# TensorE's instruction pieces in the hand-made schedule of a retention layer with an MLP: visits placed by piece, one group at a time

## The chip, the core and the metric

The kernel runs on one core of a Trainium2 chip. The metric is the device time of one execution in microseconds (us); the time of a kernel is the median of its runs. Five engines work side by side and meet at semaphores: TensorE (PE in the profile, with its weight loads as PEld), VectorE (DVE), ScalarE (ACT), GpSimd (POOL) and SyncE (SP). Each carries out its own instructions in the order in which the program has them.

## The reference

Retention over 8 batches x 8 heads x 576 positions x 64 dimensions, then an MLP with an exact GELU over all 4608 tokens (512 -> 2048 -> 512). Inputs and output are float32; the kernel computes in bfloat16 with float32 sums.

```python
scores = scale * np.matmul(q, k.transpose(0, 1, 3, 2))
gamma = 1.0 - 2.0 ** (-5.0 - np.arange(H, dtype=np.float32))
rel = pos[:, None] - pos[None, :]
Dmat = np.where(rel >= 0, gamma[:, None, None] ** rel[None, :, :], 0.0)
attn = np.matmul(scores * Dmat, v)
x = attn.transpose(0, 2, 1, 3).reshape(B * S, H * D)
h = x @ w_in
out = (0.5 * h * (1.0 + erf(h / sqrt(2)))) @ w_out
```

## The kernel before

**Attention.** The sequence is cut into four chunks of 128 positions and a tail of 64. A *unit* is one chunk of one batch with all eight heads (the tails of two batches share one). The first four units are groups of their own; after them a *group* is two units, the same chunk of two batches, and a tail is a group too: 22 groups, 0 to 21. A group passes through four matmul steps, each of many small matmuls that use a part of TensorE's rows or columns:

- scores (`scores`, L559): 32 matmuls for a group; VectorE then multiplies the mask on (`masked`, L592)
- inner (`inner`, L646, tails L631): masked scores times v, 32 matmuls for a group (16 for a tail)
- state (`state`, L661): the sum over keys and values that the next chunk needs, 32 matmuls; VectorE and ScalarE keep it (L666 to L689)
- cross (`cross`, L711): q times the state of the chunk before, 32 matmuls, left out in chunk 0; VectorE then scales the result into x (`evacuate`, L735)

Inner, state and cross of a group together are a *visit* (`attend`). A visit may hold two groups: then the inner steps of both come first, their states next, their cross steps last. The planner ties two groups into one visit when they have the same chunk, from group `VISIT` on, and when the attention leads the MLP by more than `LEAD` units.

q and k must be turned before the scores. The groups in `BY_PE` (4 and 5, since `NPE = 2`) are loaded with positions on partitions, in 128 KB loads, and turned by TensorE: `turn`, 8 transposes for each of q and k (L494), then a copy out of PSUM. They need no second load of k. The groups in `BY_DVE` are loaded in four smaller loads for each of q and k (L342), turned by VectorE (`turn_dve`, L514) and, for q, put in order by ScalarE (`apart`, L525); their state step needs k once more, untransposed (`kn_ld`, L348). ScalarE scales v for all groups from 4 on (`scaled_v`, L609).

**MLP.** Tokens stand in 9 blocks of 512 = 4 units. The first product is plain for blocks 0 to 5 (`mlp1`, L758: matmuls of 128, 256 or 512 tokens) and a form with 7 products in place of 8 for blocks 6 to 8 (`mlp1_fast`, L972). The second product is plain for a part of block 0 (`mlp2`, L791) and has 7 products after it (`mlp2_fast`, L862: 8 matmuls of 256 columns per product). ScalarE applies the GELU; VectorE makes the sums that the 7-product forms need.

**The order.** All is one program without a loop on the chip. While it is built, a planner (the `while True` loop at the end) keeps a clock for each engine in `T`, with an assumed duration for each step, and at each moment takes a step whose inputs are there by these clocks: attention steps that are due first, then MLP work, which fills what is left. Attention steps are `A` (a visit), `AA` (a double visit), `U` (a state step by itself), `S` (scores) and `T` (transposes by TensorE). `AHEAD` and `RATE` bound how far scores may run ahead of the MLP, `SB`, `PER_G` and `PER_B` order VectorE's side jobs. So each engine's order is fixed when the program is built; on the chip an engine only waits.

Loads are issued by GpSimd in the order of the list `ORDER` (L374), and group by group after it (`reload`); stores by SyncE.

Of the kernel before, what the change touches and what calls it, by code (L numbers as in the profile page):

```python
# [17 lines left out]
def kernel(  # L18
# [14 lines left out]
    nc = tc.nc  # L33
# [35 lines left out]
    PLAIN = 4  # L69
    NPE = 2  # L70
    FAST1 = (5, 6, 7, 8)[PLAIN // 4:]
# [366 lines left out]
    def release(b, when):  # L438
        held.remove(b)
        free_at[b] = when  # L440

    def pe(dur, to="full"):
# [38 lines left out]
    def turn(n, jj):  # L481

        qk = loaded[groups[n][0]][0][jj]
        if n < 4:
            b, t = bank([128, HP, 128], BF16, "qk_ps")
            dst, m = turned(n, jj), HP
            for x in range(HP):
                nc.tensor.transpose(t[:, x], qk[:, 2 * x:2 * x + 2, :], ident1)
        else:
            b, t = bank([128, H, 128], BF16, "qk_ps")  # L490
            dst, m = turned(n, 1) if jj else qk.rearrange("p (h s) -> p h s", h=H), H
            for y in range(2):
                for hp in range(HP):
                    nc.tensor.transpose(t[:, y * HP + hp], qk[:, 4 * D * hp + y:4 * D * hp + 4 * D:2], ident1)  # L494
# [44 lines left out]
    def scores(n):  # L539
        g = groups[n]  # L540
        if n < 4:
            qT, kT = turned(n, 0), turned(n, 1)
            got = bank_pair(128)
            for hp in range(HP):
                for e in range(2):
                    sl = slice(64 * e, 64 * e + 64)
                    nc.tensor.matmul(got[1][:, e, hp, :], lhsT=kT[sl, hp, :], rhs=qT[sl, hp, :],
                                     start=True, stop=True)
            st[g[0]]["sc"] = got, pe(0.23, "row")
        else:  # L550
            short = len(g) == 1
            got = [bank_pair(TAIL if short else C) for _ in g]
            for hp in range(HP):
                for y in range(2):
                    for e in range(2):
                        for j in range(2):
                            sl = slice(64 * e + 32 * j, 64 * e + 32 * j + 32)
                            dst = got[0][1][64 * j:64 * j + 64, e, hp, :] if short else got[j][1][:, e, hp, :]
                            nc.tensor.matmul(dst, lhsT=turned_k(n, sl, hp, y), rhs=turned_q(n, sl, hp, y),  # L559
                                             start=(y == 0), stop=(y == 1), skip_group_check=True)  # L560
# [61 lines left out]
    def inner(i):  # L622
        bp, ci, j = units[i]
        s = st[i]
        if j is None:
            s["o"] = o = bank_pair(TAIL)
            for h in range(H):
                for jj in range(2):
                    sl, e = slice(64 * jj, 64 * jj + 64), 64 * (h % 2)
                    y = h // 2 + HP * (h % 2)  # L630
                    nc.tensor.matmul(o[1][e:e + 64, jj, h // 2, :], lhsT=s["vh"][sl, h, :], rhs=s["ret"][y // HP][sl, y % HP, :],  # L631
                                     start=(h < 2), stop=False, skip_group_check=True)
            s["B"] = pe(0.25, "quad")
            s_done.add(i)
        else:
            if i in raw:
                s["o"] = bank([128, HP, 128], FP32, "o_ps")
                o = s["o"][1]
            else:
                s["o"] = bank_pair(C) if j == 0 else st[i - 1]["o"]  # L640
                o = s["o"][1][:, j]
            vals = values(i) if i in raw else s["vh"]
            for hp in range(HP):
                for z in range(4):
                    e, d0 = z // 2, z % 2 * 32
                    nc.tensor.matmul(o[32 * z:32 * z + 32, hp, :], lhsT=vals[:, 2 * hp + e, d0:d0 + 32], rhs=s["ret"][e][:, hp, :],  # L646
                                     start=(hp == 0), stop=(ci == 0 and hp == HP - 1), skip_group_check=True)
            s["B"] = pe(0.27, "col4")
            if j == 1 and ci < NCI - 1:
                u_due.append((bp, ci))  # L650

    def state(bp, ci):
        pair = pair_of[bp, ci]
        b, u_ps = bank([128, H, D], FP32, "u_ps")
        for hp in range(HP):
            for y in range(2):
                for e in range(2):
                    for j, i in enumerate(pair):
                        h, p0 = 2 * hp + e, 64 * e + 32 * j
                        keys = loaded[i][0][1][:, h, y::2] if i < 4 else loaded[i][2][:, j, h, y::2]  # L660
                        nc.tensor.matmul(u_ps[p0:p0 + 32, 2 * hp + y, :], lhsT=keys, rhs=st[i]["vh"][:, h, :],  # L661
                                         start=(hp == y == 0), stop=(hp == HP - 1 and y == 1), skip_group_check=True)
# [36 lines left out]
    def cross(n):  # L699
# [6 lines left out]
        for hp in range(HP):  # L706
            for y in range(2):
                for e in range(2):
                    for j in range(2):
                        sl = slice(64 * e + 32 * j, 64 * e + 32 * j + 32)  # L710
                        nc.tensor.matmul(o[64 * e:64 * e + 64, j, hp, :], lhsT=u[sl, 2 * hp + y, :], rhs=turned_q(n, sl, hp, y),  # L711
                                         start=False, stop=(hp == HP - 1 and y == 1), skip_group_check=True)
# [41 lines left out]
    def mlp1(t, m0, n, lo, hi):  # L754
        b, hT = bank([128, n, hi - lo], FP32, "hT")
        for m in range(m0, m0 + n):
            for cc in range(N_DM):
                nc.tensor.matmul(hT[:, m - m0, :], lhsT=w_in[:, cc, m * 128:m * 128 + 128], rhs=x_tiles[t][:, cc, lo:hi],  # L758
                                 start=(cc == 0), stop=(cc == N_DM - 1))
# [25 lines left out]
    def mlp2(t, ts, m0, m1):  # L785
# [4 lines left out]
        for m in range(m0, m1):  # L790
            nc.tensor.matmul(oT, lhsT=g_of(t, ts // 2)[:, m, cols], rhs=w_out[:, m, :], start=(m == 0), stop=(m == N_DF - 1))  # L791
        done = pe((m1 - m0) * 0.2158)
# [58 lines left out]
    def mlp2_fast(t, p, name):  # L851
# [9 lines left out]
        for kk in range(HK):  # L861
            nc.tensor.matmul(dst, lhsT=x[:, kk, :], rhs=y[:, kk, :], start=(name in "125" and kk == 0),  # L862
                             stop=(kk == HK - 1), skip_group_check=True)
# [91 lines left out]
    def mlp1_fast(t, i, name):  # L955
# [13 lines left out]
        for m in range(2):  # L969
            for cc in range(HC):  # L970
                c0 = (2 * i + m) * 128
                nc.tensor.matmul(dst[:, m, :], lhsT=a[cc][:, c0:c0 + 128], rhs=y[:, cc, :],  # L972
                                 start=(name in "125" and m == 0 and cc == 0), stop=(cc == HC - 1), skip_group_check=True)
# [218 lines left out]
    def warm(n):  # L1192
        b, t = bank([128, 512], FP32, "warm")
        for _ in range(n):
            nc.tensor.matmul(t, lhsT=zeros[:, :128], rhs=zeros, start=True, stop=True)
        pe((0.32 if T["pe"] < HOT else 0.2158) * n)
# [34 lines left out]
    for _ in range(N_WARM):  # L1231
        b, t = bank([128, 512], FP32, "warm")
        nc.tensor.matmul(t, lhsT=zeros[:, :128], rhs=zeros, start=True, stop=True)
        release(b, 0.0)
    T["pe"] = 1.3 + 0.62 * N_WARM
    while True:
# [18 lines left out]
        if nB < nA:  # L1255
# [5 lines left out]
            if tied:  # L1261
                both = 1e9
                if nA > groups[n + 1][-1]:
                    both = max(ready, ready_for(n + 1))
                    acts.append((max(both, free_time(len(g) > 1 and units[g[0]][1] < NCI - 1, out_pairs(n, n + 1))), "AA"))
# [12 lines left out]
        if nT < 4 + NPE and nT <= group_of[min(nA, N_U - 1)] + 3 and (nT < 4 or not half or ring_free("tk")):  # L1278
# [99 lines left out]
```

## Time and profile before

| | |
|---|---|
| time, median of 3 runs | 292.36 us (291.45 to 294.36) |
| the profiled execution: time, span | 293.79 us, 292.0 us |
| TensorE busy | 277.5 us (95%), 4155 recorded matmuls |
| VectorE / ScalarE / GpSimd busy | 230.4 / 180.2 / 136.0 us |
| granted TensorE clock | full in all slices |
| loads (queue q0) | 21.12 MB, landing until 170.7 us |

In the profile "span" is the time from the first to the last instruction. A timeline line gives start and length in us, engine, source line, operation, what is written <- what is read, the shape and the number of instructions merged into it, and in brackets the idle time before it with its releaser. "issue" as a releaser means that the profile knows of nothing that the engine waited for. Matmuls overlap, so that a step is best measured from its start to the start of the next.

### The profile page before, as it was taken

The page shows a single profiled execution, that of the slowest core. Times are in us where ns is not written, and L with a number is a line of the kernel's source. Part 1 is how long each engine was busy: PE and PEld are TensorE (multiplying, and loading weights), DVE is VectorE, ACT ScalarE, POOL GpSimd, SP SyncE. Part 2 cuts the span into 40 slices and gives each one's busy share as a digit, 9 for nine tenths or more (in the row PEclk, how much of TensorE's full clock was granted, in tenths as well). Part 3 has the DMA queues.
Part 4 walks back from the last instruction along what each step waited for, and adds up shares of the span by engine and source line. Part 5 has one row for each costly group of instructions (what it writes and reads, how often), then busy time and mean ns, then how long its engine had stood idle before and what let it go on. Part 6 is the DMA issues. An engine that isn't in the chain of part 4 may idle for free.

```text
span 292.0 us, 9753 instructions
## 1 busy us (share of the span) xinstructions
PE 277.5 (95%) x4155; PEld 212.3 (73%) x4179; DVE 230.4 (79%) x380; ACT 180.2 (62%) x407; POOL 136.0 (47%) x205
## 2 busy tenths in 40 slices
PE   6979998999899999999799999999999999999994
PEld 2468766888747666665666766767888888888883
DVE  5564387899959579877797898988996998899851
ACT  7456558579778687679477596744545455556421
POOL 8956867989899777787785900000000000000000
PEclk9999999999999999999999999999999999999999
DMA  9999999999999999999999750201010202101114
GB/s 154 170 188 191 195 154 211 185 151 127 144 108 120 126 191 148 164 131 186 131 129 175 61 93 3 57 21 72 2 74 0 75 0 75 72 2 72 38 54 127
DMA packets 109131, 31.96 MB, mean 109 GB/s; under 512 B 85792, under 2 KB 104736, under 8 KB 109088
## 3 DMA queue, kind: packets, MB, share of 16 engines
q0 software_dynamic: 100400, 21.12, 82.6%
q1 hardware_dynamic: 7184, 9.44, 9.8%
q10 hardware_dynamic: 1504, 0.79, 1.0%
q8 instruction: 32, 0.52, 0.7%
q14 instruction: 11, 0.09, 0.1%
HBM read 42.99 MB, written 9.44 MB: 180 GB/s over the span
## 4 chain that ended last, share of the span: by engine, by line
PE 89%; POOL 4%; DMA 3%; issue 2%; ACT 0%; DVE 0%; POOLq 0%
PE psum L862 36%; PE psum L758 27%; PE psum L972 13%; DMA early<-in_v_dram 3%; PE psum L559 3%; PE psum L646 3%; PE psum L711 3%; PE psum L791 2%; POOL early L364 2%; PE psum L661 1%; POOL w_in L307 1%; PE psum L494 1%; PE psum L631 0%; POOL w_out L322 0%; ACT x L453 0%
## 5 line engine op out<-in xcount | busy, mean ns | idle before, releaser
L758 PE MATMUL psum<-x,w_in 128*128 128x512 bf16 (+2 forms) x547 | 89.7, 307 | 2.8 <-issue 1.7
L758 PEld LDWEIGHTS <-w_in 128*128 128x128 bf16 x568 | 49.8, 98 | 24.1 <-issue 1.2
L862 PEld LDWEIGHTS <-g_all 128*128 128x128 bf16 x544 | 52.3, 98 | 12.8 <-issue 2.0
L763 ACT ACTIVATE g_all<-psum 128x512 bf16<-128x512 f32 x64 | 37.6, 594 | 28.2 <-PE psum L758 28.2
L862 PE MATMUL psum<-w_out,g_all 128*128 128x256 bf16 x408 | 52.0, 273 | 1.9 <-issue 1.8
L862 PEld LDWEIGHTS <-s 128*128 128x128 bf16 x408 | 39.5, 98 | 8.8
L342 POOL DMA_DIRECT2D k_ld<-in_k_dram x64 | 35.2, 567 | 18.4 <-DMA q_ld<-in_q_dram 7.8
L609 ACT ACTIVATE vh<-v_ld,dv 128x128 bf16<-128x128 bf16 (+1 forms) x144 | 42.2, 380 | 0.0
L977 ACT ACTIVATE g_all<-t 128x512 bf16<-128x512 f32 x36 | 22.6, 630 | 29.0 <-DVE t L985 28.9
L592 DVE TENSOR_TENSOR ret<-psum,msk 128x1024 bf16<-128x1024 f32 (+1 forms) x32 | 35.6, 1150 | 3.0 <-PE psum L559 2.5
L342 POOL DMA_DIRECT2D q_ld<-in_q_dram x64 | 35.1, 566 | 1.8 <-DMA q_ld<-in_q_dram 0.9
L862 PE MATMUL psum<-wt,s 128*128 128x256 bf16 x272 | 34.1, 273 | 0.0
L848 DVE TENSOR_TENSOR o_sb<-psum,t 128x256 f32<-128x256 f32 x51 | 21.5, 421 | 14.9 <-PE psum L862 6.0
L453 ACT COPY t<-psum 128x256 f32<-128x256 f32 (+1 forms) x46 | 20.0, 435 | 17.1 <-PE psum L862 13.4
L985 DVE TENSOR_TENSOR t<-psum,t 128x512 f32<-128x512 f32 x36 | 24.7, 689 | 6.0 <-ACT t L453 4.2
L972 PE MATMUL psum<-x,w_in 128*128 128x256 bf16 x192 | 25.9, 273 | 0.0
L451 DVE COPY t<-psum 128x512 f32<-128x512 f32 (+1 forms) x41 | 22.7, 559 | 3.7 <-PE psum L862 3.6
L766 ACT ACTIVATE g_all<-psum 128x512 bf16<-128x512 f32 (+1 forms) x39 | 19.1, 523 | 10.4 <-PE psum L758 9.8
L735 DVE TENSOR_TENSOR x<-psum,dqT 128x1024 bf16<-128x1024 f32 (+1 forms) x18 | 19.3, 1099 | 2.1 <-PE psum L711 2.1
L972 PEld LDWEIGHTS <-w_in 128*128 128x128 bf16 x192 | 18.8, 98 | 2.4
L972 PE MATMUL psum<-x,ws 128*128 128x256 bf16 x144 | 19.5, 273 | 0.0
L353 POOL DMA_DIRECT2D v_ld<-in_v_dram x14 | 16.3, 1164 | 3.5 <-DMA kn_ld<-in_k_dram 1.3
(107 smaller groups left out, 371.4 us busy)
## 6 DMA issues: line engine op xcount, KB each, us to landing
out_dram<-o_sb SPq DMA_DIRECT2D x31, 256.0 KB, 2.3
v_ld<-in_v_dram POOLq DMA_DIRECT2D x14, 256.0 KB, 5.6
q_ld<-in_q_dram POOLq DMA_DIRECT2D x48, 64.0 KB, 5.1
k_ld<-in_k_dram POOLq DMA_DIRECT2D x48, 64.0 KB, 4.2
kn_ld<-in_k_dram POOLq DMA_DIRECT2D x12, 256.0 KB, 6.4
w_in<-in_moe_w_in_dram POOLq DMA_DIRECT2D x8, 256.0 KB, 8.4
w_out<-in_moe_w_out_dram POOLq DMA_DIRECT2D x8, 256.0 KB, 9.2
q_ld<-in_q_dram POOLq DMA_DIRECT2D x4, 128.0 KB, 9.2
```

The costliest lines, as they stand in the source:

```text
L342: nc.gpsimd.dma_start(qk["qk".index(what)][p0:p0 + 32, 0:HP * per].rearrange("p (h x) -> p h x", h=HP), {"q": q, "k": k}[what][2 * bp + jj ...
L451: nc.vector.tensor_copy(dst, src)
L453: nc.scalar.copy(dst, src)
L592: nc.vector.tensor_tensor(both.rearrange("p (e h) s -> p e h s", e=2), t, by, op=ALU.mult)
L609: nc.scalar.activation(vh[:, 0:m, h], src[:, :, h], AF.Copy, scale=dv[:, h, ci:ci + 1])
L758: nc.tensor.matmul(hT[:, m - m0, :], lhsT=w_in[:, cc, m * 128:m * 128 + 128], rhs=x_tiles[t][:, cc, lo:hi], start=(cc == 0), stop=(cc == N ...
L763: nc.scalar.activation(g_all[:, t % 2, :, m0, :], hT.rearrange("p n (a c) -> p (n a) c", a=2), AF.Gelu)
L848: nc.vector.tensor_tensor(dst, src, f[key], op=ALU.add)
L862: nc.tensor.matmul(dst, lhsT=x[:, kk, :], rhs=y[:, kk, :], start=(name in "125" and kk == 0), stop=(kk == HK - 1), skip_group_check=True)
L972: nc.tensor.matmul(dst[:, m, :], lhsT=a[cc][:, c0:c0 + 128], rhs=y[:, cc, :], start=(name in "125" and m == 0 and cc == 0), stop=(cc == HC ...
L977: nc.scalar.activation(g_of(t, part)[:, m0:m0 + 2], src, AF.Gelu)
L985: nc.vector.tensor_tensor(f[key], f["b"][1], f[key], op=ALU.add)
```

## The change

The planner gets a model of how TensorE's instructions come. It counts the instructions (`mm` and `mm_turn` stand for the matmul and transpose calls, 2.004 instructions each), takes them to come in pieces of 256 whose edges lie at 194 plus a multiple of 256, and takes a piece to be there `FETCH` = 5.0 us after the piece before it was begun. From 20 us on, its TensorE clock `pe` stands still at an edge until then, and a visit or a score step that would cross an edge is not due before that time (`fetch_at`). These are waits in the planner's clock: no wait instruction is added to the program; another step takes the place.

With it come other constants: one more group is turned by TensorE (`NPE` 3), no visit holds two groups (`VISIT` 30 is past the last group), one more warm-up matmul in each early gap (`WPLUS`), other bounds for how far the attention runs ahead and for the side jobs, and a new `ORDER` of the loads. In the program that results TensorE has 4188 matmuls and transposes in place of 4179.

```diff
-    NPE = 2
+    NPE = 3
-    VH_POOL = 30
+    VH_POOL = 16
-    AHEAD = 14
-    RATE = 3.8
+    AHEAD = 13
+    RATE = 4.4
-    STATE10 = 20.0
+    STATE10 = 24.0
+    FETCH = 5.0
-    WPLUS = 0
-    VISIT = 8
-    LEAD = 2.0
+    WPLUS = 1
+    VISIT = 30
+    LEAD = 5.0
-    SLACK, SB, PER_G, PER_B, TURN0 = 1.2, 9.0, 6.0, 40.0, 0.0
+    SLACK, SB, PER_G, PER_B, TURN0 = 1.2, 5.0, 10.0, 30.0, 0.0
...
-    ORDER = ("wi0 io k2 q1 k1 wi7 q2 v1 k3 wi1 wo2 v0 wi6 q3 v2 wi5 wi3 wi2 v3 q4 wi4 wo1 wo0 wo4 wo7 wo6 wo3 wo5 "
-             "k4 q5 v4 k5 q6 dq2 k6 k7 q7 v6 q8 q9 k8 n4 n8 k9 q10 v8 q11 dq3 n6 k11 q12 k10 v10 n10 q13 k13 dq4 "
-             "n12 k12 v12 dq0").split()
+    ORDER = ("wi0 io k2 q1 k1 wi7 q2 v1 k3 wi1 wo2 v0 wi6 q3 v2 wi2 wi5 wi3 v3 wi4 q4 wo1 wo0 wo4 wo3 wo7 wo6 wo5 "
+             "k4 q5 n4 v4 k5 q6 dq2 k6 k7 q7 q8 q9 v6 k8 n8 k9 q10 v8 dq3 n6 k11 k10 q11 q12 n10 v10 q13 k13 dq4 "
+             "n12 v12 dq0 k12").split()
...
+    count = [3.0, 3.0]
+    piece = [0.0]
+
+    def mm(*a, **k):
+        count[0] += 2.004
+        nc.tensor.matmul(*a, **k)
...
+    def place(n):
+        return (n - 194.0) // 256, (n - 194.0) % 256
+
+    def fetch_at(n):
+
+        at = place(count[0])[1]
+        wait = piece[0] + FETCH - (256 - at) * 0.0075 if at + n >= 256 else 0.0
+        return 0.0 if T["pe"] < 20.0 else wait
+
+    def one_piece(n):
+        return place(count[0])[1] + n < 512
+
     def pe(dur, to="full"):
...
-        T["pe"] += dur * (2.0 if T["pe"] < HOT else 1.0)
+        dur *= 2.0 if T["pe"] < HOT else 1.0
+        new, old = place(count[0])[0], place(count[1])[0]
+        if new > old:
+            turn_at = T["pe"] + dur * (1 - place(count[0])[1] / max(1.0, count[0] - count[1]))
+            wait = max(0.0, piece[0] + FETCH - turn_at) if T["pe"] > 20.0 else 0.0
+            piece[0] = turn_at + wait
+            T["pe"] += wait
+        count[1] = count[0]
+        T["pe"] += dur
         return T["pe"] + DRAIN
...
-                if nA > groups[n + 1][-1]:
+                if nA > groups[n + 1][-1] and one_piece(384 if len(g) > 1 else 192):
...
-                acts.append((max(ready, free_time(n < 4, out_pairs(n))), "A"))
+                acts.append((max(ready, fetch_at(192 if n >= 4 else 0), free_time(n < 4, out_pairs(n))), "A"))
...
-                acts.append((max(s_ready(), free_time(0, len(g))), "S"))
+                acts.append((max(s_ready(), fetch_at(64 if n >= 4 else 0), free_time(0, len(g))), "S"))
```

More of the change, by code (lines that the diff above doesn't have):

```diff
@@ L440, in release, with mm_turn @@
         free_at[b] = when
+    count = [3.0, 3.0]
[3 more added lines that the diff above has]
+        nc.tensor.matmul(*a, **k)
+    def mm_turn(*a, **k):
+        count[0] += 2.004
+        nc.tensor.transpose(*a, **k)
+    def place(n):
[6 more added lines that the diff above has]
+        return place(count[0])[1] + n < 512
     def pe(dur, to="full"):
@@ L487, in turn @@
             for x in range(HP):
-                nc.tensor.transpose(t[:, x], qk[:, 2 * x:2 * x + 2, :], ident1)
+                mm_turn(t[:, x], qk[:, 2 * x:2 * x + 2, :], ident1)
         else:
@@ L493, in turn @@
                 for hp in range(HP):
-                    nc.tensor.transpose(t[:, y * HP + hp], qk[:, 4 * D * hp + y:4 * D * hp + 4 * D:2], ident1)
+                    mm_turn(t[:, y * HP + hp], qk[:, 4 * D * hp + y:4 * D * hp + 4 * D:2], ident1)
         done = pe(0.056 * m)
@@ L630, in inner @@
                     y = h // 2 + HP * (h % 2)
-                    nc.tensor.matmul(o[1][e:e + 64, jj, h // 2, :], lhsT=s["vh"][sl, h, :], rhs=s["ret"][y // HP][sl, y % HP, :],
+                    mm(o[1][e:e + 64, jj, h // 2, :], lhsT=s["vh"][sl, h, :], rhs=s["ret"][y // HP][sl, y % HP, :],
                                      start=(h < 2), stop=False, skip_group_check=True)
@@ L645, in inner @@
                     e, d0 = z // 2, z % 2 * 32
-                    nc.tensor.matmul(o[32 * z:32 * z + 32, hp, :], lhsT=vals[:, 2 * hp + e, d0:d0 + 32], rhs=s["ret"][e][:, hp, :],
+                    mm(o[32 * z:32 * z + 32, hp, :], lhsT=vals[:, 2 * hp + e, d0:d0 + 32], rhs=s["ret"][e][:, hp, :],
                                      start=(hp == 0), stop=(ci == 0 and hp == HP - 1), skip_group_check=True)
@@ L757, in mlp1 @@
             for cc in range(N_DM):
-                nc.tensor.matmul(hT[:, m - m0, :], lhsT=w_in[:, cc, m * 128:m * 128 + 128], rhs=x_tiles[t][:, cc, lo:hi],
+                mm(hT[:, m - m0, :], lhsT=w_in[:, cc, m * 128:m * 128 + 128], rhs=x_tiles[t][:, cc, lo:hi],
                                  start=(cc == 0), stop=(cc == N_DM - 1))
@@ L790, in mlp2 @@
         for m in range(m0, m1):
-            nc.tensor.matmul(oT, lhsT=g_of(t, ts // 2)[:, m, cols], rhs=w_out[:, m, :], start=(m == 0), stop=(m == N_DF - 1))
+            mm(oT, lhsT=g_of(t, ts // 2)[:, m, cols], rhs=w_out[:, m, :], start=(m == 0), stop=(m == N_DF - 1))
         done = pe((m1 - m0) * 0.2158)
@@ L861, in mlp2_fast @@
         for kk in range(HK):
-            nc.tensor.matmul(dst, lhsT=x[:, kk, :], rhs=y[:, kk, :], start=(name in "125" and kk == 0),
+            mm(dst, lhsT=x[:, kk, :], rhs=y[:, kk, :], start=(name in "125" and kk == 0),
                              stop=(kk == HK - 1), skip_group_check=True)
@@ L1194, in warm @@
         for _ in range(n):
-            nc.tensor.matmul(t, lhsT=zeros[:, :128], rhs=zeros, start=True, stop=True)
+            mm(t, lhsT=zeros[:, :128], rhs=zeros, start=True, stop=True)
         pe((0.32 if T["pe"] < HOT else 0.2158) * n)
@@ L1232 @@
         b, t = bank([128, 512], FP32, "warm")
-        nc.tensor.matmul(t, lhsT=zeros[:, :128], rhs=zeros, start=True, stop=True)
+        mm(t, lhsT=zeros[:, :128], rhs=zeros, start=True, stop=True)
         release(b, 0.0)
```

12 lines of the change are left out of this document (6 added, 6 removed).

## The prediction

> **What bounds the kernel now.** I read the page first (busy shares and the chain that ended last), then the waits of TensorE, then its timeline around each wait, then the DMA queues and the landings of the loads.
>
> ```profile
> span 292.0 us, 9753 instructions
> PE 277.5 (95%) x4155; PEld 212.3 (73%) x4179; DVE 230.4 (79%) x380; ACT 180.2 (62%) x407; POOL 136.0 (47%) x205
> ...
> q8 instruction: 32, 0.52, 0.7%
> ...
> PE 89%; POOL 4%; DMA 3%; issue 2%; ACT 0%; DVE 0%; POOLq 0%
> ```
>
> TensorE is the chain: 89% of the span, and busy for 277.5 of 292.0 us. The rest of the chain is the start: a load of v that lands at 20.97 us releases the chain, and from there TensorE alone sets the time. Nearly the only thing on the chain after that is "issue", a stop with no releaser that the profile knows. The timeline of TensorE shows three of them:
>
> ```profile
> 48.01 0.35 PE L711 MATMUL psum<-q_ld,u_sb 32*64 32x128 bf16 x10
> 49.64 0.52 PE L711 MATMUL psum<-q_ld,u_sb 32*64 32x128 bf16 x22 [1.27 <-issue]
> ...
> 80.11 1.24 PE L758 MATMUL psum<-x,w_in 128*128 128x512 bf16 x5 [0.76 <-issue]
> ...
> 137.99 1.08 PE L646 MATMUL psum<-ret,vh 128*32 128x128 bf16 x64
> 138.90 0.70 PE L661 MATMUL psum<-vh,kn_ld 128*32 128x64 bf16 x64
> 139.53 1.09 PE L711 MATMUL psum<-q_ld,u_sb 32*64 32x128 bf16 x64
> 140.54 1.37 PE L862 MATMUL psum<-w_out,g_all 128*128 128x256 bf16 x11
> 143.76 0.71 PE L862 MATMUL psum<-w_out,g_all 128*128 128x256 bf16 x5 [1.84 <-issue]
> ```
>
> Together 1.27 + 0.76 + 1.84 = 3.87 us. Each lies in the middle of a run of equal matmuls, so no operand can be late. The instruction queue q8 explains them: 32 packets, 0.52 MB, so 16 KB each, over 8,334 recorded loads and matmuls of TensorE, one packet per 256 or so. Counted through the program's order, the stops fall on multiples of 256 instructions (plus 194), and in each case a packet landed shortly before: at 48.12 (work resumes at 49.64), 78.44 (80.11) and 142.52 (143.76). So TensorE waits for its next piece, and resumes 1.2 to 1.7 us after its packet has landed. Since one packet starts per edge passed, a piece must last as long as the next one takes to come. From edge to resumption the three took 5.5 (44.13 to 49.64), 4.6 (75.47 to 80.11) and 4.7 us (139.06 to 143.76). The attention is what empties pieces fast: the visit at 137.99 runs 192 matmuls, one and a half pieces, in 2.55 us, where 128 matmuls of L862 take 14 us.
>
> The Trainium skill ("Runtime: NRT & Kernel Launch", section "Instruction fetch mechanics") says that instructions come in 16 KiB blocks of 256 by a DMA queue of the sequencer, and that crossing into the next is mostly hidden. The block size agrees with the 16 KB packets here; "hidden" does not: 3.87 us are not. By that rule the first term below would be nothing, and the sum 294.3 instead of 291.7; it is a rival below, worked out from rows.
>
> **The change, term by term.** The order of the instructions of the changed program tells what moved. From the step at 202.1 us (first L972) to the end TensorE's order is the same in both; up to the v load of 20.97 us the loads have the same order, so this landing still pins the start (one warm matmul more and a shifted one fall into the 1.07 us that TensorE idles there). What changes lies between 22.1 and 202.1 us. I price each run of matmuls by its start-to-start time in the timeline: 0.109 us for a 256-wide matmul, 0.216 for a 512-wide, 0.056 for a 128-wide or a transpose, 0.56 for the 32 matmuls of a score step (L559), and 0.10 for entering attention work from full-size matmuls (a run of 8 of L862 lasts 0.97 instead of 0.87 before it). Summed so, the order of before ends at 283.6 us, the record at 287.9: the difference, 4.3, is the 3.87 of stops and 0.4 of rounding, so the prices hold.
>
> *1. The stops of before go: -3.87.* Scores and visits are now put only where a piece has had 5 us by the planner's clock, and double visits are gone.
>
> *2. New stops: +1.35.* In the new order, summed with the same prices, no piece is shorter than 4.76 us; twelve lie between 4.76 and 5.9 while loads still run. What a piece needs I take from all 18 edges of before between 44 and 165 us, as packet's landing plus 1.5 us minus TensorE's passing of the edge: from 1.1 to 6.7 us, ten of them above 4.2, five above 5.1. Averaging the shortfall over these 18 for each of the twelve gives 0.23 us for the shortest, 0.13 for one of 5.1, 0.05 for one of 5.7; the sum is 1.35. Bounds: nothing, if the slow packets meet long pieces, and 3.9 if the packets come late as often as they hurt before. I take 1.35, since the readings are of this kernel under the same loads.
>
> *3. Two more transposes by TensorE (NPE 3): +0.90.* The third group now has q and k turned by TensorE, 2 x 8 matmuls. The row:
>
> ```profile
> 39.01 0.61 PE L494 MATMUL psum<-ident,q_ld 128*128 128x128 bf16 x8
> 39.45 1.46 PE L791 MATMUL psum<-w_out,g_all 128*128 128x512 bf16 x6
> ```
>
> 39.01 to 39.45 is 0.45 each. They are on the chain in full. What they save is not: two stream transposes of VectorE (0.94 us mean each) and a 1.04 us copy of ScalarE, against two copies from PSUM (0.7 to 1.0 us); nine DMA issues of GpSimd (8 x 0.57 + 1.17 = 5.7 us) become four (4 x 0.88 = 3.5). VectorE and ScalarE never wait for a load after 26 us, so TensorE's work hides all of it. The DMA engines gain little: 1024 packets of 512 bytes at 62 ns and 2048 of 128 bytes at 32 give 129 us over 16 engines, 4096 of 128 bytes 131. By landings the old form took 5.3 us (46.38 to 51.70), four loads of the new form 3.0 (at 0.75 each, 42.08 to 44.32). Later loads come 1 to 2 us earlier.
>
> *4. Single visits: +1.28.* A single visit against half a double one:
>
> ```profile
> 75.17 0.63 PE L646 MATMUL psum<-ret,vh 128*32 128x128 bf16 x32
> 75.63 0.42 PE L661 MATMUL psum<-vh,kn_ld 128*32 128x64 bf16 x32
> 75.97 0.64 PE L711 MATMUL psum<-q_ld,u_sb 32*64 32x128 bf16 x32
> 76.55 1.05 PE L862 MATMUL psum<-wt,g_all 128*128 128x256 bf16 x8
> ```
>
> Two singles: 2 x (76.55 - 75.17) + 2 x 0.10 = 2.95. One double: 140.54 - 137.99 + 0.10 = 2.65. So 0.30 each for the three doubles with L711, 0.18 for the one without (1.81 against 1.63), 0.10 for each of the two tail pairs: 0.90 + 0.18 + 0.20.
>
> *5. Places of scores, chunk sizes: +0.08.* Two entries more from full-size work, one fewer elsewhere (+0.10); eight 256-wide matmuls of the first block replace sixteen 128-wide (-0.02). VH_POOL has no effect, since ScalarE scales v for every later group.
>
> The other loads' new order costs nothing if the loads still come in time, so that is the cover to test. By the sum the attention now runs 2 to 12 us earlier: the scores of the first late group at 98.8 instead of 105.9, a later one at 117.6 instead of 126.3. Their loads landed in before at 93.1 and 111.1, so 5.7 and 6.5 us remain, plus the 1 to 2 us of term 3. Before itself ran a score step 5.8 us after its last load (51.70 to 57.48) without a wait. Two turns on VectorE (2 x 1.13) and ScalarE's copy (1.04) need 3.3 us. The tightest new place is the k transpose of the third group, 50.6 us by the sum: q of it should land at 45.8, v of the second at 47.9, its own k at 49.4 (0.75 a load, 2.06 for v). With 1.03 a load, the longest of that run, it is 50.5. No queue is moved past another: GpSimd issues all loads in both, SyncE's stores stay.
>
> Sum: -3.87 + 1.35 + 0.90 + 1.28 + 0.08 = -0.26, span 291.7. The profiled execution took 293.79, 1.79 around its span, 1.43 above the median of 292.36. Against the median: 292.1.
>
> **Rivals.**
> *A. The waits do not take the stops away.* Either the stops are no fetches, or packets come 1 us later than the plan thinks. For it: readings above 5 us are five of 18, and the 6.7 one stood right behind a visit. Against it: all three stops lie on piece edges. Then 3.9 us stay and 2.26 are added: 292.36 + 2.3 = 294.7.
> *B. Slower: a score step meets its loads.* The loads are paced by the DMA engines (digit 9 in the page's DMA row until 165 us), and by packet time the third group's cost them the same as before. If the landings do not move and the chain of VectorE and ScalarE takes 8 to 9 us as a rule (the other scores with VectorE's turns had 7.5 us and more in before), the score steps at 73 to 118 us, several of them with 5.7 to 6.5 us, wait 2 to 3 us, once, as all later work shifts with them. It decides from a lead under about 6 us; VectorE, standing in the same wait, holds up the sums queued behind. 292.1 + 3 = 295.1. Against: the lead of 5.8 that was enough.
> *C. Faster: no piece is late at all*, and TensorE's order ends as summed: 292.36 - 3.87 + 2.26 = 290.7; with the 0.4 of rounding also gained, 290.3. For it: most pieces have over 5.4 us, and late in the kernel the packets come within 3.6 us.
>
> **How the numbers follow.** Forecast 0.54, A 0.14, B 0.17, C 0.15. A measurement of this kernel can tell about 1%, 2.9 us. The forecast (290.8 to 293.7 by the bounds of terms 2 and 3) stays within it but for 0.03 on either side; A by 0.11 of its 0.14; B is beyond for 0.12; C for 0.09. So faster 0.12, same 0.70, slower 0.18. The range 289.6 to 295.0 leaves out the far ends of B and C.
>
> **What would show it.** Right: TensorE's busy time up by about 2 us, "issue" waits under 2 us in total, visits of 32 matmuls each in about 1.5 us with the entry, L494 with 48 matmuls, first L972 at about 202 us, q8 with 32 or 33 packets. Wrong: "issue" stops of 3 us or more (A), score steps or their turns waiting for DMA (B), a chain in which the first L972 comes before 199.5 us or after 205.

## The result: 294.85 us, slower by 0.6%, and the profile after

| | before | after |
|---|---|---|
| time, median of 10 runs each | 293.02 us (291.45 to 295.83) | 294.85 us (293.41 to 296.92) |
| ratio, 95% interval | | 1.006 [1.0034, 1.0087] |
| the profiled execution: time, span | 293.79, 292.0 us | 294.77, 293.0 us |
| TensorE busy | 277.5 us | 280.9 us |

The change is within the 1% that the prediction took as the least that a measurement can tell, but its interval lies clear of 1: the kernel became slower by about 1.8 us (1.0 to 2.5), where a gain of 0.3 us was forecast. (The median of before from ten runs is 0.66 us above the one from three that the prediction started from.) Ratios, and the counts of timed executions further down, leave out the few that took over 1.5% longer than the fastest of the same kernel.

The page of the changed kernel, the lines that answer to those of before:

```profile
span 293.0 us, 9764 instructions
...
PE 280.9 (96%) x4159; PEld 213.7 (73%) x4188; DVE 224.8 (77%) x375; ACT 182.5 (62%) x410; POOL 133.9 (46%) x200
...
PEclk9989999999999999999999999999999999999999
...
q8 instruction: 32, 0.52, 0.7%
...
PE 90%; DMA 3%; POOL 3%; issue 1%; DVE 1%; ACT 0%; POOLq 0%
```

TensorE is still the chain, and busy for 3.4 us more. "issue" went from 2% of the chain to 1%, but VectorE, which had 0%, has 1% now. The third digit of the clock row fell to 8; in before all were 9. The waits of TensorE (columns: engine, tile and line, releaser, then us in total, times, longest) say which waits these are. In the changed kernel every matmul carries L449 and every transpose L453, the lines of the two helpers, so one has to go by tiles and times:

```profile
PE psum L449 <- DMA w_in<-in_moe_w_in_dram: 2.2, 1, 2.2
...
PE psum L449 <- DVE ret L625: 1.1, 1, 1.1
PE psum L449 <- issue: 0.6, 4, 0.2
```

Of the stops without a releaser, 3.87 us in three places in before, none is left: the 0.6 us are four gaps of at most 0.2 us, and gaps of 0.16 us stand in before as well. So the change did what it says. But a wait of 1.1 us for VectorE's masked scores (`ret`) is new, and the longest wait is one of 2.2 us for a load of w_in in the first 20 us. The new wait in the timeline of TensorE, inside the visit of the second double-unit group:

```profile
48.66 0.62 PE L449 MATMUL psum<-q_ld,kT 32*128 32x128 bf16 x32
...
50.19 0.63 PE L449 MATMUL psum<-ret,vh 128*32 128x128 bf16 x32
51.94 0.42 PE L449 MATMUL psum<-vh,k_ld 128*32 128x64 bf16 x32 [1.11 <-DVE ret L625]
52.28 0.64 PE L449 MATMUL psum<-q_ld,u_sb 32*64 32x128 bf16 x32
```

50.19 to 51.94 is 1.75 us for an inner step that takes 0.46 elsewhere: 1.29 us lost, at nearly the place where before lost its 1.27 (the cross step at 49.64). The start of the kernel, as windows (us of the window, then busy time and number of instructions of PE, PEld, DVE, ACT, POOL, then granted clock, DMA share and GB/s):

```profile
16.40:19.80 3.40, 1.23 (x16) 0.99 (x15) 0.00 (x0) 1.74 (x4) 1.20 (x3) 1.00 1.95 177
19.80:23.20 3.40, 3.29 (x43) 2.49 (x41) 1.97 (x4) 1.18 (x2) 2.64 (x4) 0.50 1.51 193
```

In the first window TensorE does 1.23 us of work in 3.40, since it stands for the third chunk of w_in; in the second the granted clock is half.

**The sum from the trace.** I cut the span of TensorE in three: the *start*, up to the first plain matmul run after the fourth single-unit score (22.11 us in before); the *middle*, up to the first L972; and the rest. The middle is again priced by start-to-start rows, and what it lasted above its price is the *excess*, that is, stops and waits. From the first L972 to TensorE's last matmul both kernels take 85.75 us.

| us | before | after | difference | forecast |
|---|---|---|---|---|
| start | 22.11 | 22.69 | +0.58 | 0 |
| middle, priced work | 175.86 | 178.11 | +2.25 | +2.26 |
| middle, excess | 4.15 | 2.24 | -1.91 | -2.52 |
| the rest | 85.75 | 85.75 | 0 | 0 |
| sum | | | +0.93 | -0.26 |

The agreement of the priced work is no test of the prices: the same prices were put on the same order before and after the result. The excess takes up whatever they have wrong, in this table and in the experiments. A split that needs no prices, and by which the work did not come out, follows the experiments.

### The profile page after: what moved, and what is told of

Same layout as the page of the kernel before. It is cut to its first block, busy times and chain, and to the rows that moved or that the text cites. A ratio compares the mean times of both kernels' runs of the same rounds, so it can differ in the third digit from the quotient of the medians.

```text
span 293.0 us, 9764 instructions
## 1 busy us (share of the span) xinstructions
PE 280.9 (96%) x4159; PEld 213.7 (73%) x4188; DVE 224.8 (77%) x375; ACT 182.5 (62%) x410; POOL 133.9 (46%) x200
## 4 chain that ended last, share of the span: by engine, by line
PE 90%; DMA 3%; POOL 3%; issue 1%; DVE 1%; ACT 0%; POOLq 0%
PE psum L449 89%; DMA w_in<-in_moe_w_in_dram 3%; POOL early L365 2%; PE psum L453 1%; POOL w_in L308 1%; DVE ret L625 1%; POOL w_out L323 0%; ACT x L486 0%; DVE o_sb L881 0%; POOL val L185 0%; POOL pos L187 0%; POOLq L185 0%; POOLq L1395 0%
## 5 line engine op out<-in xcount | busy, mean ns | idle before, releaser
L449 PE MATMUL psum<-x,w_in 128*128 128x256 bf16 (+2 forms) x725 | 119.0, 301 | 3.9 <-DMA w_in<-in_moe_w_in_dram 2.2
L449 PEld LDWEIGHTS <-w_in 128*128 128x128 bf16 x752 | 68.1, 98 | 27.0 <-DMA w_in<-in_moe_w_in_dram 2.3
L449 PEld LDWEIGHTS <-g_all 128*128 128x128 bf16 x576 | 55.5, 98 | 14.9
L449 PE MATMUL psum<-w_out,g_all 128*128 128x256 bf16 (+1 forms) x439 | 59.1, 280 | 0.1
L449 PEld LDWEIGHTS <-s 128*128 128x128 bf16 x408 | 39.5, 98 | 9.2
L343 POOL DMA_DIRECT2D k_ld<-in_k_dram x60 | 33.2, 577 | 23.3 <-DMA kn_ld<-in_k_dram 8.2
L449 PE MATMUL psum<-wt,s 128*128 128x256 bf16 x272 | 34.5, 273 | 0.1
L343 POOL DMA_DIRECT2D q_ld<-in_q_dram x60 | 33.1, 579 | 1.4 <-DMA q_ld<-in_q_dram 0.5
L768 DVE TENSOR_TENSOR x<-psum,dqT 128x1024 bf16<-128x1024 f32 (+1 forms) x18 | 19.8, 1102 | 0.7 <-PE psum L449 0.7
L449 PE MATMUL psum<-x,ws 128*128 128x256 bf16 x144 | 19.5, 273 | 0.0
L449 PE MATMUL psum<-wt,g_all 128*128 128x256 bf16 x136 | 17.5, 273 | 0.0
L449 PE MATMUL psum<-w_out,s 128*128 128x256 bf16 x136 | 17.5, 273 | 0.0
```

The costliest lines, as they stand in the source:

```text
L343: nc.gpsimd.dma_start(qk["qk".index(what)][p0:p0 + 32, 0:HP * per].rearrange("p (h x) -> p h x", h=HP), {"q": q, "k": k}[what][2 * bp + jj ...
L449: nc.tensor.matmul(*a, **k)
L768: nc.vector.tensor_tensor(x.rearrange("p m (j s) -> p j m s", j=2), o, by, op=ALU.mult)
```

## The experiments

Timed kernels had five rounds beside before on the same chip; their ratios are to before, with the 95% interval. The others have one profile. The first theory, *start*, was that the halved clock and the w_in wait come with `WPLUS` and the new order. The second, *fetch*, was that the stops removed had come back in other places. Rivals stand in the expectations.

**1. The changed kernel without the extra warm-up matmuls**

```diff
-    WPLUS = 1
+    WPLUS = 0
```

> The changed kernel with WPLUS = 0 again; TensorE's order after the start is the same, matmul for matmul. Theory 'start': the one warm matmul more at 6.7 us brought the full clock at 9.5 us instead of 13.0, TensorE reached the third w_in chunk at 16.9 us, stood 2.17 us for its load, and the clock then fell to half from 19.8 to 23.2 us. Without it the granted clock has no row of 0.5 before the end, the first half of the start ends 0.8 us sooner (second 256-wide step of the first product at 22.6 instead of 23.4 us), and the time is 0.8 us under the changed kernel's, about 1.003 of before. Theory 'middle': the start is noise between executions and the loss lies in the transposes and single visits; the time stays at 1.006 of before.

Measured: 295.53 us, ratio 1.0046 [1.0021, 1.0071]. In its profile the clock stays full in the same window, yet the wait for w_in (2.1 us) stays too:

```profile
16.40:19.80 3.40, 1.26 (x16) 1.02 (x15) 0.00 (x0) 1.46 (x4) 1.15 (x3) 1.00 1.94 177
19.80:23.20 3.40, 3.11 (x56) 2.61 (x55) 2.60 (x5) 1.57 (x3) 2.58 (x4) 1.00 1.52 192
```

The start ends at 21.68 us there, a whole us earlier than in the changed kernel, and the time isn't measurably better: its interval overlaps that of the change.

**2. Before with the extra warm-up matmuls**

```diff
-    WPLUS = 0
+    WPLUS = 1
```

> The kernel before with WPLUS = 1 and nothing else. Theory 'start': the clock falls to half between 19.8 and 23.2 us here too, mean granted clock 0.994, and the time rises by 0.8 us, 1.003 of before. Theory 'middle': 1.000 of before within its interval, no row of 0.5 in the clock, or one that costs nothing.

Measured: 294.56 us, ratio 1.0022 [0.9994, 1.005]; full clock, start 21.67, and stops at the three places of before (1.04, 0.91 under the name of VectorE, and 1.23 us) and a fourth of 0.56 us at 160.8. With `WPLUS` 1 there is no halved clock here, and further down the order of before with `WPLUS` 0 has one. So *start* falls.

**3. The model of the pieces alone: the planner of the change with all constants and the load order of before**

```diff
-    NPE = 3
+    NPE = 2
...
-    WPLUS = 1
-    VISIT = 30
-    LEAD = 5.0
+    WPLUS = 0
+    VISIT = 8
+    LEAD = 2.0
...   (and VH_POOL, AHEAD, RATE, STATE10, SB, PER_G, PER_B and ORDER as before)
```

> The new planner code (piece model, FETCH = 5.0) with all constants and the load order of before: two groups turned by TensorE, double visits from group 8 on, no more warm matmuls. Priced by the rows of before, TensorE's order without stops ends 0.2 us later than that of before; pieces under 5 us are 4.0, 4.2, 4.3, 4.9 and 5.0. Theory 'pieces': the stops of 3.9 us fall to 1 to 2 us, time 0.993 of before (0.990 to 0.997). Rival 'the model does nothing for the time', the stops come back in other places: 1.000.

Measured: 292.52 us, ratio 0.997 [0.9947, 0.9993]: faster than before, if by little, and 0.9% below the change. Its priced work is 0.20 us above that of before and its excess 2.69:

```profile
PE psum L449 <- DMA w_in<-in_moe_w_in_dram: 2.3, 1, 2.3
...
PE psum L449 <- DVE x L768: 0.9, 1, 0.9
PE psum L449 <- issue: 0.7, 2, 0.4
```

The stops fall from 3.87 us to 0.7 at almost no work, and 0.9 us come back as a wait for VectorE's x. So the model pays; what loses lies in the other parts.

**4. The changed kernel with no time for a fetch in the planner**

```diff
-    FETCH = 5.0
+    FETCH = 0.0
```

> The changed kernel with FETCH = 0, so that the planner never waits for a piece; three groups turned by TensorE, single visits, loads and warm matmuls as in the changed kernel. Priced by rows, its order without stops ends 0.1 us before the changed kernel's; it has pieces of 4.1, 4.6, 3.3, 2.7, 4.3 and 4.2 us. Theory 'pieces': stops with no releaser of 3 to 6 us in all come back, and the time is 2 to 4 us above the changed kernel's, 1.013 to 1.02 of before. Rival 'the model does nothing': the same time as the changed kernel, 1.006.

Measured: 301.86 us, ratio 1.0266 [1.0234, 1.0298], more than was expected of it. The profile is of the fastest of its six executions (299.63 us); its excess is 7.8 us. Its waits, and then one of them in the timeline:

```profile
PE psum L449 <- issue: 5.1, 4, 1.6
```

```profile
49.74 0.41 PE L449 MATMUL psum<-q_ld,u_sb 32*64 32x128 bf16 x15 [1.62 <-issue]
```

The priced work is that of the change (178.01 against 178.11 us); only the places of its parts differ. So the planner's allowance keeps most of 5.1 us of stops away, as it should if the stops are the pieces. It also shows that single visits and a third group of transposes don't by themselves lessen the stops.

**5. The changed kernel with the score step of group 5 held until the visit of group 4 is done**

```diff
-            if T["dve"] <= now + SB and nA - nB <= 2:
+            if T["dve"] <= now + SB and nA - nB <= 2 and not (n == 5 and nB < nA):
```

> The changed kernel, with the score step of group 5 kept back until the visit of group 4 has run (in the changed kernel it stands before it, and the state step of that visit then stands still until VectorE has masked those scores, 50.8 to 51.9 us). Priced by rows the order is 0.1 us shorter; the fourth piece begins 5.2 us after the third and the sixth 4.6 after the fifth. Theory 'bank': the stop was only the wait for the PSUM bank that the mask frees; it goes, no other takes its place, TensorE's time beyond the priced order falls by about 1.1 us, and the time is 0.996 to 0.998 of the changed kernel's, 1.002 to 1.004 of before. Theory 'piece under the bank': the packet landed at 50.54, 1.4 us before the state step ran; a stop with no releaser appears near the fourth edge, and the time stays at 1.005 to 1.006.

This takes the `ret` wait's cause away: VectorE gets the masked scores in time. Measured: ratio 1.0071 [1.0034, 1.0108], nothing gained. The same visit in its timeline:

```profile
49.00 0.63 PE L449 MATMUL psum<-ret,vh 128*32 128x128 bf16 x32
49.45 0.42 PE L449 MATMUL psum<-vh,k_ld 128*32 128x64 bf16 x32
50.92 0.64 PE L449 MATMUL psum<-q_ld,u_sb 32*64 32x128 bf16 x32 [1.05 <-issue]
```

The wait for `ret` is gone and a stop without a releaser, 1.05 us long, stands one step later. So a late piece lay under the wait of the changed kernel: there its packet landed at 50.54, and with 1.2 to 1.8 us from landing to resumption, as at the other stops, TensorE could go on between 51.8 and 52.3. VectorE's `ret` ended at nearly the same time (49.33 + 2.36 = 51.69):

```profile
49.33 2.36 DVE L625 TENSOR_TENSOR ret<-psum,msk 128x1024 bf16<-128x1024 f32 x2 [0.18 <-PE psum L449]
```

TensorE resumed at 51.94. The profile names one releaser; two came together.

**6. Before with single visits only**

```diff
-    VISIT = 8
+    VISIT = 30
```

> The kernel before with VISIT = 30 and nothing else: single visits all through, no piece model. Priced by rows its order is 1.4 us longer (the prediction's term 4). Its pieces no longer include those of 3.2 and 3.3 us around the double visits at 120 and 138 us; 4.1, 4.6, 4.2 and 4.5 us remain. Theory 'sum': +1.4 of work, -1.8 for the stop at 142 us, the others as before: the profile shows the stops at 48 and 79 us and none near 142, time 0.997 to 1.001 of before. Rival 'single visits are the loss': the 1.4 us stand alone, 1.004 to 1.006.

Measured: ratio 1.0012 [0.9985, 1.0039], no difference. Priced work +1.38 (the prediction had +1.28), the stop of 1.84 us behind the double visit at 142 gone, excess 2.50. The stop at 48 us, where the order is still that of before, is almost gone too: the cross step there takes 0.87 us in place of 0.57. Of its waits:

```profile
PE psum L758 <- issue: 1.9, 3, 1.3
```

As far as one profile and the timing tell, what single visits save in stops they cost in work.

**7. to 9. The same kernels again: before once, after twice**

> The kernel before once more, to see how far TensorE's stops and its start differ from execution to execution. Theory 'start is chance': the full clock comes at another time than 13.0 us, the plain part of the start ends somewhere between 21.4 and 23 us; TensorE's time beyond the priced order lies between 3.5 and 5 us, with stops in the same three places. Rival 'the profiled execution of before was an odd one': stops elsewhere or under 3 us.

> The changed kernel once more. Theory 'stops vary': TensorE's time beyond the priced order, 2.2 us in the first profile, is 2 to 4 us, with stops of 0.2 to 1 us in changing places, since the packets do not come equally fast; the start ends between 21.4 and 23 us. Rival 'the first profile is typical': 2.2 us again, at the same place (50.8 us), and the start at 22.7.

> The changed kernel a third time. Theory 'the early visits': TensorE's time beyond the priced order is 2 to 3 us, and 1 us or more of it lies between 46 and 56 us, as in both earlier profiles, whatever releaser the profile names. Rival 'chance': none of it there.

The program of before a second time: span 293.6 us (before: 292.0), start 22.96 with half the clock from 19.19 to 22.61 us, excess 4.93 (before: 4.15). The three stops lie at the same places, one with another length: in the second visit it has 0.47 us in place of 1.27. Two are new, 0.44 us at 61.1 and 0.87 at 161.5:

```profile
PE psum L862 <- issue: 1.8, 1, 1.8
...
PE psum L661 <- issue: 1.1, 2, 0.9
PE psum L711 <- issue: 0.5, 1, 0.5
```

The changed program a second time: span 292.5, start 21.73, excess 2.57. Its loss lies before the visit, at the place that the prediction called tightest, where the third group is turned:

```profile
46.06 1.04 PE L449 MATMUL psum<-w_out,g_all 128*128 128x256 bf16 x8
47.99 0.61 PE L453 MATMUL psum<-ident,q_ld 128*128 128x128 bf16 x8 [0.89 <-DMA q_ld<-in_q_dram]
```

And a third time: span 294.3, excess 4.54, as much as before's, with the stops back:

```profile
PE psum L449 <- issue: 2.9, 5, 0.9
```

So one profile of each was too few: the excess of one program moves by 0.8 us (before) and 2.3 us (after) between executions.

**10. The model alone with a longer fetch**

```diff
-    FETCH = 5.0
+    FETCH = 6.5
...
-    LEAD = 2.0
+    LEAD = 5.0
```

> The piece model with the constants and loads of before, as in the run with the model alone, but FETCH = 6.5 in place of 5.0 and LEAD = 5 in place of 2. Priced by rows its order is 0.4 us longer than that of before and 0.2 longer than the model alone; only two pieces last under 5 us (4.4 and 5.0), where the model alone has five. Theory 'pieces': the late packets, 5 us and more, no longer meet TensorE at an edge; 1 to 1.5 us under the model alone, 0.991 to 0.995 of before. Rival 'what is left are other waits' (banks, copies, loads around 46 to 56 us): no better than the model alone, 0.997.

This is the kernel of experiment 3 with more room. Measured: ratio 1.0047 [1.0023, 1.0072], worse than 3. Of its waits no line says "issue" any more, but:

```profile
PE psum L449 <- DVE x L768: 2.2, 1, 2.2
...
PE psum L449 <- ACT g_all L799: 0.7, 1, 0.7
```

The first is at 54.63 us, straight behind the second visit: the MLP's next block needs that visit's x, and TensorE has nothing else to do.

**11. and 12. The change with two groups turned by TensorE, and with double visits**

```diff
-    NPE = 3
+    NPE = 2
```

> The changed kernel with NPE = 2 again: 16 transposes of TensorE fewer, the third group turned by VectorE, its loads in the old form. Priced by rows the order is 1.1 us shorter than the changed kernel's; one piece of 3.4 us appears near 54 us. Theory 'work in full': the 1.1 us come back less 0.5 of stops, 1.003 to 1.005 of before. Theory 'third group': the changed kernel's loss of 1.1 to 1.5 us between 46 and 52 us (bank, piece or load of q, another one in each profile) hangs on the third group's transposes and goes with them: 0.999 to 1.002, and no wait for a load or a mask there. Rival: nothing gained, 1.006.

```diff
-    VISIT = 30
-    LEAD = 5.0
+    VISIT = 8
+    LEAD = 2.0
```

> The changed kernel with VISIT = 8 and LEAD = 2 again: double visits where the planner's piece model lets them. Priced by rows the order is 1.5 us shorter; pieces of 3.2, 4.8, 4.5, 4.9, 5.0 and 4.9 us appear. Theory 'sum': 1.5 us of work gained, 1 to 1.6 us of stops added, so 1.002 to 1.006 of before. Rival 'single visits cost more than their rows' (more evacuations and bank changes): 0.999 or less.

Measured: 1.0052 [1.0026, 1.0079] and 1.0044 [1.0013, 1.0075]; neither differs from the change (1.006). The priced work falls by 1.09 and 1.48 us (the prediction had charged 0.90 and 1.28 for these two parts), and the excess rises from 2.24 to 5.83 and 4.66. One timeline line of each, the first without the third group's transposes, the second with double visits:

```profile
52.85 1.03 PE L449 MATMUL psum<-x,w_in 128*128 128x256 bf16 x8 [1.50 <-DVE x L768]
```

```profile
91.09 0.71 PE L449 MATMUL psum<-w_out,s 128*128 128x256 bf16 x5 [2.01 <-issue]
```

The second comes eleven matmuls of 256 columns behind a visit of two groups: the stop that single visits had taken away.

## Why the prediction was wrong, by its steps

**A split without prices.** The middle of an execution, less TensorE's waits of over 0.25 us in it, is the work of the order, whatever the prices say. (Several profiles have gaps of 0.16 us where the record of one matmul is missing: before has 4155 recorded matmuls to 4179 weight loads. And a wait costs some 0.2 us beyond its length in both orders, 0.94 for the one of 0.76 us in before.) The three profiles of the order of before and the four of the order of the change have the same matmuls in the same order in the middle.

| us | waits over 0.25 us | middle without them |
|---|---|---|
| order of before: before, before again, 2 | 3.88, 4.34, 3.73 | 176.13, 176.44, 176.72 |
| order of the change: after, again, a third time, 1 | 1.11, 1.19, 2.65, 1.03 | 179.25, 179.49, 180.01, 179.99 |
| 3, the model alone | 1.81 | 176.94 |
| 10, the model alone, longer fetch | 3.18 | 176.71 |
| 6, single visits alone | 1.69 | 178.05 |
| 4, the change with no time for a fetch | 6.00 | 179.82 |
| 5, the change, scores held | 1.69 | 178.89 |
| 11, the change, two groups turned | 3.96 | 178.90 |
| 12, the change, double visits | 3.48 | 177.81 |

From the first line to the second the waits fall by 2.49 us in the mean and the work rises by 3.26: +0.77. The forecast was -2.52 and +2.26.

**What held.** *The cause of the stops*: experiment 4 brings them back with the work unchanged (179.82), and experiment 3 takes most of them away. All 27 stops without a releaser of over 0.25 us in the middles of the fourteen profiles begin within three matmuls of a multiple of 256 instructions plus 194, and end 1.2 to 1.8 us after a packet has landed. So do three waits under VectorE's name; of the other fifteen waits of that length none lies within fifteen matmuls of such an edge. *Terms 1 and 2 in sum*, counting every wait: -2.52 against -2.77 in the profiled pair and -2.49 in the means, in part by luck (see term 2 below). *The later loads*: the waits of the changed kernel, above, have no line for a load of q or k, and the end is unchanged; rival B, which wanted 2 to 3 us from such a wait, did not come. Its nearest kin is the 0.89 us wait for q at 47.1 us, in one profile of three.

**Terms 3 to 5 failed: the work, +2.26 forecast, +3.26 found.** The parts, by the table: single visits 1.6 us (6 against before) to 1.9 (12 against the change) where term 4 had 1.28; the third group 0.8 (11) where term 3 had 0.90; the places that the model alone gives 0.5 (3) where term 5 had 0.08. One mistake shows in the rows. Term 4 gave each pair of tails only 0.10 us for one more entry into attention work. A double tail in before, then a single one in after:

```profile
197.62 0.45 PE L631 MATMUL psum<-ret,vh 64*64 64x64 bf16 x32
...
198.64 1.05 PE L862 MATMUL psum<-wt,g_all 128*128 128x256 bf16 x8
```

```profile
184.71 0.32 PE L449 MATMUL psum<-ret,vh 64*64 64x64 bf16 x16
...
185.33 1.05 PE L449 MATMUL psum<-wt,g_all 128*128 128x256 bf16 x8
```

The double one takes 1.02 us for two groups, the single one 0.62 for one: 2 x 0.62 + 2 x 0.10 against 1.02 + 0.10, so 0.32 for a pair. Two pairs make term 4 1.72 in place of 1.28, and the three terms 2.70. The other 0.56 us of the 3.26 I have not found in rows.

**Term 2 had the sum but not the place.** In twelve of the fourteen profiles 0.85 us or more is lost between 46 and 56 us, under "issue" (before, 2, 4 and 5 among them), VectorE's masked scores (after, 12), a q load (after again) or VectorE's x (3, 10, 11). Eight of them (before, after, after a third time, 1, 2, 4, 5 and 12) are one and the same late piece. Its packet belongs to the edge that TensorE passes at about 44 us, and the wait stands at the next edge; the two waits put down to the masked scores stand there too, and end 1.4 and 1.55 us after the packet. By the rows the changed order has 5.5 us of work between these edges, for which term 2 had less than 0.1 us of stop. The next piece was ready (packet's landing plus 1.5 us) 6.9, 5.4, 6.5 and 6.4 us after the edge in the four profiles of that order. Over all profiles the packet lands 3.9 to 5.6 us after the edge (mean 4.9) in the seven with three groups turned by TensorE, and 2.0 to 4.1 (mean 3.4) in the seven with two; experiment 11, which differs from the change in nothing else, has the 2.0. So "under the same loads", the ground on which term 2 averaged the readings of before, doesn't hold there: the third group's new loads come with a later packet. By what way they delay it no run shows. Term 1, for its part, took the 1.27 us of before's profile at 49.64; the same order up to there lost 1.27, 0.47, 1.04 and 0.3 us in four profiles (before, before again, 2, 6).

In 3, 10 and 11, where two groups are turned, the timelines show another wait at this place: after these visits TensorE turns to the next block's first product (x, w_in), which needs the x that these visits make. In experiment 10 that wait is 2.20 us, more than all waits of experiment 3 (1.81). That x is late because the planner holds a visit back for its piece is my reading; no run isolates it.

*A packet is often later than 5 us.* The prediction read ten of 18 needs above 4.2 us and five above 5.1, and the plan has 5.0. Over 164 piece edges between 44 and 165 us in nine profiles (packet's landing plus 1.5 us, minus TensorE's passing of the edge) the mean is 4.2 us, 27% are above 5 and 8% above 6, the longest 7.3. The average of 1.35 us for term 2 was a fair reading of this (all waits of the changed order, stops or not, are 1.03 to 2.65 us), but the third profile of after shows its spread: 2.9 us of "issue" from the same program. A longer allowance did not help (experiment 10).

**The start was not pinned.** I wrote that the v load at 20.97 us pins the start in both. It ends at one of two places: 21.4 to 22.1 us, or 22.7 to 23.1 in the executions whose clock halves for 3.41 us from about 19.2 to 19.8 us on. Both occur with both orders (before again, after) and with both values of `WPLUS`, so I take the +0.58 of the profiled pair as the chance of the two executions. The profiles in which the clock halves again after its first rise show a mean granted clock of 0.991 to 0.994, the others 0.999 or 1.0; a mean below 0.995 was read in 39 of 71 timed executions of before, in 7 of 10 of the change and in 6 of 12 of experiment 1.

**Two slips in the numbers of the prediction.** The 294.3 us for fetches that are hidden takes term 2 as nothing too, not the first term alone. And the bound of 3.9 us for term 2 gives 292.1 + 2.55 = 294.7 as the forecast's upper end, not 293.7; what was measured lies beside it.

**What stays open.** The middles give +0.77 us in the mean of the profiles, the profiled pair +0.93 with its start, the timing +1.0 to +2.5. Single executions of one program scatter by about 1 us, and the spans of the three profiles of before's order (mean 292.6) lie above those of its timed executions (291.7), while the four of the changed order (293.1) do not lie above the timed ones of the change (293.1). So the stops of before cost about 0.9 us less in a typical execution than in the profiled ones if the whole of this is stops, and their fall is then nearer 1.6 to 1.8 us than 2.5. The 294.7 of rival A ("packets come 1 us later than the plan thinks") is nearest in number; as a mechanism it holds for the edge at 44 us, but most stops did go, and experiment 4 shows what would be there without the plan.

## What to carry to other kernels

Start-to-start rows price the work of an order only as far as every kind of step has its own row: the tails, priced by the entry alone, cost three times what was charged. A profile checks such a sum without prices, as its time less its waits. A change that trades certain work (here 3.3 us of transposes, single visits and a new order) for uncertain stops (here 1.0 to 2.7 us left of 3.7 to 4.3, by which executions are compared) should be split, and its cheap part kept: the model of the pieces alone gave 0.997 [0.9947, 0.9993]. Before a stop is booked as a gain, ask what else TensorE could run at that place; in experiments 3 and 10 part of the time returned under another releaser. And take several profiles of one program before a difference under 1 us in a stall is read as the change's.

## What the runs showed of the hardware that I had not expected

**Small matmuls outrun the instruction fetch.** A visit and a score step use up a piece of 256 instructions in about 2 us (1.38 + 0.56), and with the DMA engines busy the next needs 4.2 us in the mean and up to 7.3. With the constants of the change, an order that ignores this took 2.0% longer than one that allows 5 us (1.0266 against 1.006 of before, experiment 4). The need also moves with the program: at one edge the packet landed 2.0 us after it with two groups turned by TensorE (experiment 11), and 3.9 to 5.6 with three.

**One idle stretch at the start can halve the clock.** In the changed kernel TensorE idles 2.17 us before 19.22 us, and the granted clock is 0.5 from 19.79 to 23.20 us, 3.41 us. The full clock begins between 4.1 and 13.0 us in the profiles, and its stretches last 10.24, 269.65, 279.89, 286.72 or 290.13 us, whole multiples of 3.41; so it is granted in windows of 3.41 us whose phase is another one in each execution. Counted in such windows from the start of the full clock, TensorE was busy for 0.33 to 0.38 of the window before the half clock in the five profiles that halve at about 19 to 20 us. In experiment 1 an idle time of the same length fell on two windows, busy for 0.50 and 0.79, and the clock stayed full. (One window of 0.53, right after the first rise in experiment 12, was followed by half the clock, while others of 0.50 to 0.54 were not, so no sharp limit shows.) The Trainium skill ("TensorE: Matmul & The Clock Gate", section "Part 1: The HAM clock gate (the "warmup" mystery)") describes a free-running window of about 3413 ns that halves the clock after an idle one; the length agrees with the 3.41 us here, and that an idle time shorter than the window can be enough is seen only in the trace.
